# The written-out orders of five engines, laid out anew for the second part of a gated linear attention with a ReLU-gated FFN behind it

## The chip, the cores and the metric

One core of one Trainium2 chip. The metric is the device time in microseconds of one execution, the median of several runs. TensorE is called PE, VectorE DVE, ScalarE ACT, GpSimd POOL, and SyncE, whose only work here is to issue DMAs, SP.

## The reference

Four batches, eight heads, 768 time steps, head width 48. For each batch and head a state of 48 x 48 decays by a gate and takes up one outer product per step; the query reads it. The result, 3072 rows of 384, goes through an FFN of width 1536 whose gate is a ReLU.

```python
f = 1.0 / (1.0 + np.exp(-f_logit))
for t in range(S):
    state = f[:, :, t, :, None] * state + np.einsum('bhd,bhe->bhde', k[:, :, t], v[:, :, t])
    y[:, :, t] = np.einsum('bhd,bhde->bhe', q[:, :, t], state)
x = y.transpose(0, 2, 1, 3).reshape(B * S, H * D)
out = (np.maximum(x @ w_gate, 0.0) * (x @ w_val)) @ w_out
```

## The kernel before

**Tiles.** The recurrence is computed in chunks of 128 steps: inside a chunk as masked products of scaled q and k, between chunks through the state. A tile is one chunk of one batch; there are 24, in six groups of four. Tiles of groups 0 and 1 take two neighbouring chunks of the same batch together; from group 2 on a group is one chunk c of all four batches b. The FFN works on a group at a time, 512 rows, in 12 slices of its width (j = 0 to 11).

**Operations and their names.** Every operation is one entry of a plan, with a name, the buffers that it reads and writes, and the engines that can do it. For tile cb (group c, position b):

- L: a load of f, k, q or v by DMA; `Lk3.2` is k of chunk 3 for batches 2 and 3 (384 KB).
- ef, ln (ACT): the gate's logarithm. cum (PE, L503): its running sum. eq, ek, dc (ACT, from the sum's PSUM bank): the exponentials that scale q and k, and the decay.
- hq, hk (POOL or DVE): scaled q and k. xh (SP): a crossbar transpose of both by DMA. v (POOL, DVE or ACT): v in its padded layout.
- s (PE, L584): scores, here of two tiles at once into four PSUM banks (s30 is for tiles 30 and 31). m (DVE, L592): four masks for two tiles (m300, m301 for tile 30; m310, m311 for tile 31), each 128x512.
- y (PE, L752 and L756): the result of a tile, from the old state and from the masked scores; it needs both masks of its tile. kv (PE, L772), ss (DVE), sd (POOL or DVE): the new state.
- n (ACT or DVE, L597): y copied out of PSUM. xx (SP, L616): its crossbar transpose, into xT.
- g, u (PE, L792): gate and value products of one slice of a group (`g20.3`: group 2, slice 3), three matmuls each; they need the xT of all four tiles. r (ACT L797 or DVE L798): ReLU. p (DVE, L800): the product, into gT.
- o (PE, L813): output products of a tile over four slices (`o20.4`: slices 4 to 7), which need those p. d (ACT or DVE): copy out of PSUM. S (SP, L823): the store.

**What sets the order.** `ORDER` gives each engine the list of operation indices that it runs, in that order; `~60100` and the like on PE are fillers (matmuls on zeros). `BANKS` gives the PSUM bank, out of eight, of each accumulation in the order of PE. `link` and `lay_out` find the dependencies: a reader waits for its writers, a writer for earlier readers of the same buffer, and an operation that opens a bank for everything that still reads the last tenant. An engine waits at an operation until all of these are done, and what stands behind it on that engine waits too; that holds for the queue of SP, where a load behind a store or a transpose is not issued before them. The lists come from a planner outside the kernel, which lays them out by assumed durations; the durations stand in the code (`dve_`, `act_`, the pair in `by(...)`, the two numbers in `dma(...)`), but at run time nothing reads them. Only `ORDER`, `BANKS` and the dependencies act.

**Buffers that matter here.** Three output buffers (osb), so d of one tile waits for the store three tiles earlier; two xT; four places for loads of f and of v, five for k and for q.

**Two parts.** In the first (to about 56 us) tiles of groups 0 and 1 are computed; the second part begins with `g10.0` on PE, at 55.6 us.

Of the kernel before, what the change touches and what calls it, by code (L numbers as in the profile page):

```python
# [68 lines left out]
    ],  # L69
# [46 lines left out]
class Plan:  # L116
# [5 lines left out]
    def add(self, name, ways, reads=(), writes=(), key=0.0, opens=(), after=(), follows=()):  # L122
        op = Op(len(self.ops), name, ways, reads, writes, opens, key, after, follows)
        self.ops.append(op)
        return op
# [116 lines left out]
def bass_hgrn2_outer__then__ffn_reglu_kernel(  # L242
# [10 lines left out]
    B, H, S, D = q.shape  # L253
# [32 lines left out]
    osb = [sb(f"osb{i}", [128, DM], F32) for i in range(NO)]  # L286
# [13 lines left out]
    add = pl.add  # L300
    gp, ve, sc, te, sy = nc.gpsimd, nc.vector, nc.scalar, nc.tensor, nc.sync
# [20 lines left out]
    def by(e, emit, t):  # L322
        return {e: (emit, t[0], t[1], "")}
# [479 lines left out]
    def ffn_out(g, b):  # L803
        gi, oi = g % NG, (g * B + b) % NO
        P = (g + 1) * B * 10 + 5 + NJ * 3 + b * 3
        last = g == NC - 1 and b == B - 1
        cuts = [(0, 256), (256, DM)] if last else [(0, DM)]
        for x, (e0, e1) in enumerate(cuts):
# [8 lines left out]
            odst = osb[oi][:, e0:e1]  # L817
# [4 lines left out]
            dst = bass.AP(tensor=out.tensor, offset=(bt * S + ch * C) * DM + e0, ap=[[DM, C], [1, e1 - e0]])  # L822
            op = add(f"S{g}{b}" + "ab"[x] * last, by("SP", lambda odst=odst, dst=dst: sy.dma_start(dst, odst), (0.36, 0.36)), [f"osb{oi}_{x}"] + ([f"osb{oi}_1"] if x == 0 and not last else []),  # L823
# [119 lines left out]
```

## Time and profile before

| | us |
|---|---|
| median of three runs | 196.28 |
| the runs | 195.69, 196.28, 198.73 |
| the profiled execution | 197.44 |
| its span, first to last instruction | 195.7 |
| granted clock of TensorE | 1.00 throughout |

| stage (us from the span's start) | PE busy | DVE busy | ACT busy | DMA share |
|---|---|---|---|---|
| 55.4 to 79.4 (24.0) | 23.69 | 19.96 | 15.97 | 0.91 |
| 79.4 to 86.0 (6.6) | 5.72 | 5.17 | 4.12 | 0.66 |
| 86.0 to 110.2 (24.2) | 22.90 | 19.73 | 11.38 | 0.94 |
| 110.2 to 140.0 (29.8) | 28.97 | 22.45 | 12.96 | 0.97 |
| 140.0 to 169.5 (29.5) | 28.42 | 19.42 | 9.28 | 0.50 |
| 169.5 to 195.7 (26.2) | 23.27 | 13.35 | 5.54 | 0.16 |

A matmul's busy time contains its way through the array, which overlaps with the next one, so a busy PE can still lose time between two matmuls; the distance between starts tells it. The DMA share is the mean over 16 DMA engines of the time that their packets took, and can exceed 1 where packets overlap. A load of 384 KB issued by SP lands between 5.1 and 5.9 us after its issue at the median, the transpose into xT after 2.7, the transpose of scaled q and k after 3.6, a store after 2.2.

### The profile page before, as it was taken

How to read it: one execution, taken by the hardware profiler on the slowest of the kernel's cores; microseconds unless marked ns; L12 is line 12 of the kernel's file. 1: busy time of each engine (PE TensorE's matmuls, PEld its weight loads, DVE VectorE, ACT ScalarE, POOL GpSimd, SP SyncE). 2: the span in 40 equal slices, each digit the busy share in tenths (PEclk: the TensorE clock that was granted, in tenths of full speed). 3: DMA queues.
4: the chain of work that ended last, by engine and by line, in shares of the span. 5: the costliest groups of instructions: out<-in, count | busy, mean ns of one | idle time of the engine just before them, and what ended most of it. 6: DMA issues, size and time to landing. Idle time of an engine off the chain costs nothing.

```text
span 195.7 us, 4619 instructions
## 1 busy us (share of the span) xinstructions
PE 185.2 (95%) x1858; PEld 109.7 (56%) x1881; DVE 141.1 (72%) x266; ACT 88.4 (45%) x190; POOL 53.7 (27%) x83
## 2 busy tenths in 40 slices
PE   7998999999999999989989898999998999999994
PEld 7554675555655556655555455566544556555563
DVE  4486947997859797877896767997348976277621
ACT  2776962511689923464227684226077012122120
POOL 8858402901407830106121705014006000000000
PEclk9999999999999999999999999999999999999999
DMA  6999999999999895969998799995593711410013
GB/s 152 325 284 208 153 201 269 213 214 283 245 202 223 191 164 114 202 149 197 222 218 178 154 232 143 238 224 117 156 284 71 111 40 24 163 59 0 0 46 118
DMA packets 113638, 33.21 MB, mean 170 GB/s; under 512 B 106832, under 2 KB 113360, under 8 KB 113616
## 3 DMA queue, kind: packets, MB, share of 16 engines
q1 hardware_dynamic: 102576, 27.01, 63.9%
q0 software_dynamic: 3776, 3.54, 11.5%
q10 hardware_dynamic: 7264, 2.36, 4.6%
q8 instruction: 15, 0.25, 0.5%
q14 instruction: 7, 0.06, 0.1%
HBM read 25.95 MB, written 4.72 MB: 157 GB/s over the span
## 4 chain that ended last, share of the span: by engine, by line
PE 66%; DMA 11%; DVE 8%; ACT 6%; issue 4%; SPq 2%; POOL 1%; DVEq 0%; ACTq 0%
PE ps L792 34%; PE ps L813 20%; DMA f_in<-in_f_logit_dram 9%; DVE gT L800 4%; DVE relu L798 2%; PE ps L584 2%; DMA xT<-xn 2%; PE ps L756 1%; PE ps L752 1%; PE ps L503 1%; ACT relu L797 1%; ACT expo L516 1%; ACT expo L518 1%; PE ps L672 1%; DVE hats L541 1%
## 5 line engine op out<-in xcount | busy, mean ns | idle before, releaser
L800 DVE TENSOR_TENSOR gT<-relu,ps 128x512 bf16<-128x512 bf16 (+1 forms) x76 | 48.8, 654 | 19.7 <-ACT relu L797 10.9
L792 PE MATMUL ps<-xT,wg 128*128 128x512 bf16 (+1 forms) x218 | 56.0, 368 | 2.2 <-DMA xT<-xn 1.6
L792 PE MATMUL ps<-xT,wv 128*128 128x512 bf16 (+1 forms) x219 | 56.2, 368 | 0.5
L813 PE MATMUL ps<-wo,gT 128*128 128x384 bf16 (+2 forms) x300 | 51.8, 320 | 0.0
L797 ACT ACTIVATE relu<-ps 128x512 bf16<-128x512 f32 (+1 forms) x43 | 24.9, 582 | 49.2 <-DVE gT L800 24.1
L813 PEld LDWEIGHTS ps<-wo,gT 128*128 128x128 bf16 x300 | 27.4, 98 | 17.4 <-DVE gT L800 0.6
L792 PEld LDWEIGHTS ps<-xT,wv 128*128 128x128 bf16 x228 | 23.6, 108 | 19.9
L792 PEld LDWEIGHTS ps<-xT,wg 128*128 128x128 bf16 x228 | 23.1, 108 | 20.4 <-DMA xT<-xn 1.9
L540 POOL TENSOR_TENSOR hats<-q_in,expo 128x384 bf16<-128x384 f32 x15 | 15.6, 1050 | 39.8 <-ACT expo L518 28.6
L798 DVE TENSOR_SCALAR relu<-ps 128x512 bf16<-128x512 f32 (+1 forms) x33 | 21.0, 645 | 3.9 <-PE ps L792 3.5
L592 DVE TENSOR_TENSOR ptm<-ps,tri 128x512 bf16<-128x512 f32 x32 | 20.7, 682 | 2.9 <-PE ps L584 2.8
L820 DVE COPY osb<-ps 128x384 f32<-128x384 f32 (+1 forms) x14 | 7.5, 536 | 12.2 <-PE ps L813 6.7
L570 POOL CAST vpad<-v_in 128x384 bf16<-128x384 f32 x9 | 5.0, 562 | 38.1 <-DMA v_in<-in_v_dram 38.1
L540 POOL TENSOR_TENSOR hats<-k_in,expo 128x384 bf16<-128x384 f32 x12 | 12.0, 1011 | 12.1 <-ACT expo L516 11.9
L819 ACT ACTIVATE osb<-ps 128x384 f32<-128x384 f32 (+1 forms) x11 | 5.3, 478 | 21.9 <-PE ps L813 15.4
L478 ACT ACTIVATE f_in<-f_in 128x768 f32<-128x768 f32 x12 | 10.1, 841 | 8.1 <-DMA f_in<-in_f_logit_dram 8.1
L518 ACT ACTIVATE expo<-ps 128x384 f32<-128x384 f32 x24 | 11.6, 493 | 2.9 <-PE ps L498 1.6
L516 ACT ACTIVATE expo<-ps 128x384 f32<-128x384 f32 x24 | 11.6, 492 | 2.4 <-POOL hats L540 1.7
L597 ACT ACTIVATE xn<-ps 128x384 bf16<-128x384 f32 x11 | 5.3, 487 | 14.0 <-PE ps L756 14.0
L877 PE MATMUL ps<-zeros 128*128 128x100 bf16 (+1 forms) x80 | 11.0, 310 | 0.5 <-issue 0.3
L657 DVE TENSOR_TENSOR ptm<-ps,tmask 128x512 bf16<-128x512 f32 x16 | 10.1, 681 | 0.2 <-PE ps L650 0.2
L481 ACT ACTIVATE bneg<-f_in 128x768 bf16<-128x768 f32 x12 | 10.1, 841 | 0.2
(74 smaller groups left out, 170.9 us busy)
## 6 DMA issues: line engine op xcount, KB each, us to landing
f_in<-in_f_logit_dram SPq DMA_DIRECT2D x12, 384.0 KB, 5.9
out_dram<-osb SPq DMA_DIRECT2D x23, 192.0 KB, 2.2
q_in<-in_q_dram SPq DMA_DIRECT2D x11, 384.0 KB, 5.6
k_in<-in_k_dram SPq DMA_DIRECT2D x11, 384.0 KB, 5.6
v_in<-in_v_dram SPq DMA_DIRECT2D x8, 384.0 KB, 5.1
v_in<-in_v_dram ACTq DMA_DIRECT2D x4, 384.0 KB, 7.6
wg<-in_moe_w_gate_dram POOLq DMA_DIRECT2D x2, 384.0 KB, 8.2
wv<-in_moe_w_val_dram POOLq DMA_DIRECT2D x2, 384.0 KB, 8.4
```

Source lines behind the costliest of these rows:

```text
L478: add(f"ef{c}{b0}", by("ACT", lambda: sc.activation(raw, raw, AF.Exp, scale=-1.0), act_(n)), keys, keys, key=P)
L481: add(f"ln{c}{b0}", by("ACT", lambda: sc.activation(bo, fl, AF.Ln, bias=1.0), act_(n)), keys + [f"bneg{bi}"], [f"bn{bi}_{x % 2}" for x in ...
L516: add(f"ek{c}{b}", by("ACT", lambda: sc.activation(ex[:, 1, :], bc.ap[:, 0:HD], AF.Exp, scale=1.0), act_(HD)), [bc], [f"expk{ei}"], key=P + 1)
L518: add(f"eq{c}{b}", by("ACT", lambda: sc.activation(ex[:, 0, :], bc.ap[:, 0:HD], AF.Exp, scale=-1.0), act_(HD)), [bc], [f"expq{ei}"], key=P ...
L540: return {**by("POOL", lambda: gp.tensor_tensor(o, i_, e_, ALU.mult), pool_(HD)), **by("DVE", lambda: ve.tensor_tensor(o, i_, e_, ALU.mult ...
L592: add(f"m{c}{b}{j}", by("DVE", lambda b=b, j=j, mi=mi: ve.tensor_tensor(ptm[mi][:, j, :, :], s[b, j].ap[:, :].rearrange("p (n t) -> p n t" ...
L792: z = te.matmul(bank.ap[:, 0:n], wt[:, kt, w_cols(j)], xT[xi][:, kt, n0:n1], start=(kt == 0), stop=(kt == NK - 1))
L797: add(f"r{c}{b0}.{j}", {**by("ACT", lambda: sc.activation(rdst, gate.ap[:, 0:n], AF.Relu), act_(n)), **by("DVE", lambda: ve.tensor_scalar_ ...
L798: **by("DVE", lambda: ve.tensor_scalar_max(rdst, gate.ap[:, 0:n], 0.0), dve_(n))}, [gate], [f"relu{ri}"], key=P)
L800: add(f"p{c}{b0}.{j}", by("DVE", lambda: ve.tensor_tensor(gT[gi][:, j, n0:n1], rdst, val.ap[:, 0:n], ALU.mult), dve_(n)), [val, f"relu{ri} ...
L813: z = te.matmul(o.ap[:, 0:e1 - e0], gT[gi][:, j, b * C:(b + 1) * C], wo[:, j, e0:e1], start=(j == 0), stop=(j == NJ - 1))
L877: te.matmul((op.opens[0].ap if op.opens else banks[7])[:, 0:fill % 1000], zeros[:, 0:128], zeros[:, 0:fill % 1000], start=True, stop=True, ...
```

## The change

`ORDER` and `BANKS` are replaced from a certain place on each engine; up to there every list is the same. On PE the first place that differs stands behind `g10.0`, where `u10.0` comes in front. On SP it stands behind `Lf2.2` and `S00`, where `S02` comes in front of `Lq2.0`. 79 operations move to another engine, most of them between ACT and DVE: relu 17 from ACT to DVE and 14 back, copies of y 6 and 3, output copies 3 and 7. No operation is added or dropped. One assumed duration changes, that of the issue of a store. Of the lists, cut to the first lines that differ on PE and SP, and the rows that hold the stretch around group 2's start:

```diff
@@ ORDER, PE
-        262, 294, 298, 215, 216, 217, 306, 308, 302, 388, 310, 380, 312, 326, 410, 322, 324, 338, 415, 423, 404, 328, 342,
+        262, 294, 298, 215, 216, 217, 306, 308, 302, 304, 388, 310, 380, 312, 326, 423, 415, 328, 342, 344, 410, 322, 404,
...
-        407, 366, 340, 351, 436, 367, 542, 352, 442, 357, 556, 360, 361, 550, 553, 362, 547, 561, 460, 452, 454, 569, 462,
+        357, 407, 431, 401, 350, 351, 442, 360, 361, 362, 436, 550, 556, 352, 542, 561, 569, 553, 547, 460, 462, 476, 478,
...
@@ ORDER, SP
-        46, 48, 50, 55, 53, 58, 64, 66, 59, 60, 65, 373, 371, 370, 374, 214, 372, 376, 516, 375, 518, 386, 224, 394, 517,
+        46, 48, 50, 55, 53, 58, 64, 66, 59, 60, 65, 373, 371, 370, 374, 214, 224, 372, 376, 516, 229, 375, 518, 394, 517,
...
@@ ffn_out
-            op = add(f"S{g}{b}" + "ab"[x] * last, by("SP", lambda odst=odst, dst=dst: sy.dma_start(dst, odst), (0.36, 0.36)), [...])
+            op = add(f"S{g}{b}" + "ab"[x] * last, by("SP", lambda odst=odst, dst=dst: sy.dma_start(dst, odst), (0.6, 0.6)), [...])
```

The stretch around the second pair of rows in names:

```
PE before: ... y20 u10.11 o11.4 s22 y21 o13.4 u10.9 o10.4 y22 o13.8 s30 o10.8 y23 o11.8 kv31 o12.0 o12.4
           kv30 y31 o12.8 y30 cum32 g20.3 g20.1 u20.1 cum33 u20.3 g20.7 ...
PE after:  ... y21 s22 y20 o10.0 o10.4 y23 o12.0 o12.4 o12.8 y22 kv30 kv31 o10.8 s30 cum32 cum33 y31 y30
           g20.3 u20.3 g20.7 u20.7 g20.11 u20.11 g20.0 u20.0 g20.4 u20.4 g20.8 u20.8 g20.2 ...
DVE before: ... m221 m230 m220 p10.9 m231 m310 m301 d10 v30 m311 ss31 m300 sd31 ss30 sd30 d13 r20.3 ...
DVE after:  ... m210 m211 m200 m201 m231 m230 m221 m220 n20 ss30 ss31 sd30 m311 m300 m310 m301 d13 n30 r20.3
            p20.3 r20.7 hk33 p20.7 r20.11 p20.11 p20.0 r20.4 p20.4 r20.8 p20.8 p20.1 p20.5 ss33 ...
ACT after:  ... d11 n21 n23 v30 v31 d12 n22 ef32 d10 ln32 eq32 dc33 dc32 eq33 ek32 n31 ek33 r20.0 ...
SP before:  ... S01 xh30 xh31 xx20 Lv3.0 xx21 Lf3.2 xx22 xx23 S10 S11 Lk3.2 Lq3.2 xx30 Lq4.0 Lv3.2 S13 xh32 xh33
            S12 xx31 Lk4.0 Lf4.0 Lv4.0 Lv4.2 xx32 xx33 Lf4.2 Lk4.2 ...
SP after:   ... S01 xh23 xh31 xh30 Lv3.0 Lf3.2 xx21 xx20 xx23 xx22 S10 Lk3.2 Lq3.2 Lq4.0 S13 xx30 Lv3.2 Lk4.0
            xh33 xh32 S12 xx31 Lf4.0 Lv4.0 Lv4.2 Lf4.2 Lk4.2 xx33 xx32 xh40 xh41 S11 Lq4.2 ...
```

Later places that the prediction speaks of, in the same way: on PE `u30.8 s40 g30.2`, then `s42 o32.0 u30.9 o31.0 y42 o30.0 u30.6 g30.10 y43 o32.4`; `cum51 cum50 o30.8 g40.1 u40.1 g40.5 u40.5 g40.9 u40.9 g40.2 cum53 cum52`; `y50 g40.7 u40.7 o43.0 s52 ... y53 o41.4 o40.8`. On SP the last load of f stands in `xx42 xx43 S22 Lf5.2 S32`, before in `S22 Lk5.0 Lf5.2 S30`. On DVE `s40`'s masks open a run `m400 m401 m410 p30.2 m411 r30.3 hq43 p30.3 r30.6 p30.7 v50 n41 p30.1 r30.11 p30.11 p30.5 m420 m421 m431 p30.9 m430 n42 p30.6`. On ACT `eq50 ek51 ek50 d30 r40.1 eq51 ef52 r40.5 ln52`. PE ends with `o53.4b o53.8b`, the half of 128 columns, where before it ended with `o53.4a o53.8a`, the half of 256.

More of the change, by code (lines that the diff above doesn't have):

```diff
@@ L822, in ffn_out @@
             dst = bass.AP(tensor=out.tensor, offset=(bt * S + ch * C) * DM + e0, ap=[[DM, C], [1, e1 - e0]])
-            op = add(f"S{g}{b}" + "ab"[x] * last, by("SP", lambda odst=odst, dst=dst: sy.dma_start(dst, odst), (0.36, 0.36)), [f"osb{oi}_{x}"] + ([f"osb{oi}_1"] if x == 0 and not last else []),
+            op = add(f"S{g}{b}" + "ab"[x] * last, by("SP", lambda odst=odst, dst=dst: sy.dma_start(dst, odst), (0.6, 0.6)), [f"osb{oi}_{x}"] + ([f"osb{oi}_1"] if x == 0 and not last else []),
                      [f"out{g}_{b}_{x}"], key=P)
```

72 rows, old and new, of tables (BANKS, ORDER) are left out of this document.

## The prediction

> **What bounds the kernel now.** I read the page first (busy shares, slices, chain), then who PE waits for from 55 us on, then the order of time around the largest wait, then the landing times of the DMAs. All durations are of the one profiled execution: span 195.7 us, 197.44 us with what lies around it; the median of the runs is 196.28 us.
>
> ```profile
> PE 185.2 (95%) x1858; PEld 109.7 (56%) x1881; DVE 141.1 (72%) x266; ACT 88.4 (45%) x190; POOL 53.7 (27%) x83
> ...
> PEclk9999999999999999999999999999999999999999
> ...
> PE 66%; DMA 11%; DVE 8%; ACT 6%; issue 4%; SPq 2%; POOL 1%; DVEq 0%; ACTq 0%
> ```
>
> PE sets the end at an undisturbed clock; the 11% of DMA on the chain is mostly the first load of f, which the change doesn't touch.
>
> ```profile
> PE ps L792 <- DMA xT<-xn: 1.6, 2, 0.9
> PE ps L503 <- ACT bneg L481: 0.9, 1, 0.9
> PE ps L584 <- DVE ssum L454: 0.5, 1, 0.5
> PE ps L584 <- DVE relu L798: 0.4, 1, 0.4
> PE ps L792 <- issue: 0.4, 2, 0.2
> PE ps L772 <- DVE hats L541: 0.2, 1, 0.2
> ```
>
> In the second part PE visibly waits 4.0 us, and 1.6 + 0.9 of it is for transposes and for a late load of f. A second count gives what reordering can win at all. The chain has `88.14 6.51 PE ps L792 x30`, 0.217 us a matmul, so a gate or value piece (3 matmuls) is 0.65 us; in the same way an output piece (4) is 0.65, a score piece s 0.55, y 0.37, a state product kv 0.17, a cumulative sum 0.26 (0.16 in batch 5). From g10.0 (55.6 us) to the last matmul there are 118 gate/value pieces (76.3 us at 0.647), 57 output pieces and the two narrow halves (37.1 + 2.0), 8 s (4.4), 16 y (6.0), 12 kv (2.0) and 16 sums (3.8): 131.6 us, to 187.2. The last matmul ends at 193.0, so some 5.8 us is lost. No order of the same work gains more, and a gain of over 2% (3.9 us) needs two thirds of it back.
>
> ```profile
> 79.45 0.62 PE L584 MATMUL ps<-qkT 48*128 48x128 bf16 x16
> 79.47 3.46 SPq L616 DMA_TRANSPOSE xT<-xn  x2
> ...
> 80.11 1.29 DVE L592 TENSOR_TENSOR ptm<-ps,tri 128x512 bf16<-128x512 f32 x2 [0.92 <-PE ps L584]
> ...
> 82.05 0.68 DVE L592 TENSOR_TENSOR ptm<-ps,tri 128x512 bf16<-128x512 f32 x1
> ...
> 83.11 0.68 DVE L592 TENSOR_TENSOR ptm<-ps,tri 128x512 bf16<-128x512 f32 x1
> ...
> 83.32 0.33 PE L752 MATMUL ps<-st,qkT 128*128 128x96 bf16 x4
> ...
> 84.34 0.33 PE L752 MATMUL ps<-st,qkT 128*128 128x96 bf16 x4
> ...
> 86.01 0.38 PE L792 MATMUL ps<-xT,wg 128*128 128x512 bf16 x1 [0.89 <-DMA xT<-xn]
> ```
>
> First s30, then its four masks on DVE, then y31 and y30, which read them, then g20.3, held by xx23. Between s30's end and y31 PE has 3.2 us of other work here: that hides the masks. The last transpose takes 3.99 us to land (chain: `81.75 3.99 DMA xT<-xn`); the median is 2.7, between 2.3 and 5.2.
>
> **The change part by part.** No instruction is added or removed. The 0.36 that becomes 0.6 at L823 is a planner's cost; the orders are written out, so it runs as nothing. 79 operations change engine: DVE takes 17 relu from ACT and gives 14 back, and ends 5 instructions up, some 3 us of busy time. What counts is where PE meets a wait.
>
> *Waits that go.* ln52 and cum53 (0.9): Lf5.2 was issued at 140.19, behind Lk5.0, and landed 5.03 later. Now it stands behind xx43 and S22, some 8 us of PE work ahead of cum53; 5.0 of landing, 0.9 for exp and 0.9 for log leave about a microsecond, though r40.1, eq51 and r40.5 share ACT with them. g30.1 (0.7): its transposes had 5.2 us of PE work from the last y of the batch, now 7.2. s32 (0.5): from cum32 and cum33 it had 10.0, now 14.5. s40 and kv43 (0.4 + 0.2): their places change, with slack. g50 keeps its 5.2 us, but n53 follows y53 directly. With the 0.4 of "issue" this is 3.1 of the 4.0. The 0.9 before g20.3 goes too, but see the next.
>
> *The wait that comes.* The new order of PE is y22, kv30, kv31, o10.8, s30, cum32, cum33, y31, y30, g20.3: only 0.52 us between s30 and y31, where 3.2 stood. Let s30 start at t. DVE has ss30, ss31 and sd30 (0.55 each) from kv30's result at t - 0.65, so until t + 1.0; s30's result is there at t + 0.7. Then m311, m300, m310, m301, 0.68 each: m310 ends at t + 3.05, m301 at t + 3.73. PE reaches y31 at t + 1.07 and waits 2.0; y31 takes 0.37, and y30 waits 0.3 more. g20.3 starts at t + 4.15 instead of t + 1.81: 2.3 us. Its transposes: y20's copy n20 stands behind eight masks on DVE, at about t - 2.0, then xx20, xx23 and xx22 leave SP 1.2 apart, xx22 at t + 0.45; at the median it lands at t + 3.15, hidden, at 3.99 it lands at t + 4.4 and costs 0.3. I take the median, because Lf3.2, which stood between xx21 and xx22 before, now stands ahead of all four.
>
> The Trainium skill (DMA: Bandwidth & Descriptors, Queues, rings and completion order) says that an engine takes descriptors of a ring in their order, so a load issued ahead delays a transpose. By that rule the move of Lf3.2 is right and the sum stays; the five loads that now stand ahead of xx33 would go against it, by up to the 1.3 between 3.99 and 2.7. Row and order: those five (384 KB each) need some 10 us at the 200 GB/s that the slices show, and g30.1 is 17 us of work away.
>
> *Where DVE falls behind.* From kv21 to y20 I followed ACT and DVE with the same durations: kv20 waits 0.3 for dc21 (ACT has r10.6, dc22, ek22 ahead of it), o13.0 0.25 for p10.3, o13.4 0.45 for p10.4 (p10.11, p10.5, r10.4, hq30 ahead, 2.6 us of DVE), s20, s22 and y20 0.5 together: 1.5, where this stretch lost 0.8. From s40 to o32.4 DVE has no gap: 23 instructions, 15 us, and p30.6 comes 0.6 late for o32.4. In batch 4, y50 waits 0.2 (m501), o43.0 0.3 (p40.3), o40.8 0.4 (p40.11, behind n52 and r40.11). Four further places (g10.5, s40, o32.0, u30.9) have under 0.15 us of slack; a wait that ends just in time showed 0.2 here, so I count 0.4.
>
> *Sum.* New order: 1.5 + 2.3 + 0.15 (o20.4 on p20.6) + 0.6 + 0.9 + 0.4 = 5.9, against 5.8 lost now. At the end the last copy and store are 128 columns wide instead of 256: copy 0.29 for 0.38, landing 1.6 for 1.7, 0.2 less. Span 195.6. My slack is read from busy times that ignore semaphores, which errs towards too little waiting, so I add 0.2 and leave the tail out: 195.8, or 196.4 beside the median.
>
> **The rivals.** *A, the later landing pays in full (0.14):* DVE reaches the masks early and the pinch costs 0.5 or less. Then the sum of 5.9 falls by 1.8, and without the 0.4 to 3.7, 2.1 less than is lost now; with the tail's 0.2 that is a span of 193.4 and a time of 194.0. For it: DMA is the last releaser at two of the largest waits. Against: four masks in a row are 2.7 us whatever the DMAs do.
>
> *B, slower: a load stops DVE (0.13).* hk33 now stands on DVE between r20.7 and p20.7, with all of batch 2's relu and products behind it. It needs Lk3.2, issued only after S10, about 5 us ahead of it. k loads land in 5.7 at the median, but between 3.7 and 12.1. PE goes on until u20.8 wants the bank of p20.7, some 2.4 us of slack. It decides from a landing of about 7.4 us; at 12.1 PE loses 4.7: 201.1. For it: S02 and S03 also now stand ahead of Lq2.0 and Lk2.2, and S03 waits for d03 on DVE, so these leave 1 to 3 us later. Against: Lk3.2 before, issued at 85.28, let hk32 start at 89.18, after 3.9.
>
> *C, the clock (0.03).* The trace grants full clock in all 40 slices; its longest wait of PE in the second part is 0.9, the new ones 2.0 and 0.3. If one slice of 4.9 us ran at half, 2.45 us of work is lost: 198.9. The Trainium skill (TensorE: Matmul & The Clock Gate, Why this matters for your kernels) warns of idle gaps over some 3 us; by that rule 2.0 stays short of it, and no run here shows a longer one.
>
> **How the numbers follow.** The likeliest case has 0.70, at 196.4, with its own range 194.6 to 198.6: the transpose's 0.3, the tight places and a pinch between 1.0 and 3.0. To hold 8 in 10 I reach down into A and towards C: 193.6 to 199.2. 2% is about what a measurement of this kernel can tell from no change (its runs lie between 195.69 and 198.73): faster is under 192.4, slower over 200.2. Faster needs A with most of the short waits gone as well: 0.06. Slower is B beyond a landing of 11.2 us (half of its chance, 0.06) or lags of DVE that add up in the likeliest case (0.06): 0.12. Within 2%: 0.82.
>
> **What would show it.** Right: a wait of PE for DVE ptm at L756 or L752 of about 2 us near 86, none for xT at g20.3 over 0.4, none for bneg at L503 of 0.9, and PE's last matmul within 2 us of 193. Wrong: hk33 idle for k_in with PE idle behind it (B); no wait at y31 (A); a clock under 9 (C); or a new wait on xT or qkT.

## The result and the profile after

| | before | after |
|---|---|---|
| median, same chips (us) | 197.37 | 198.30 |
| the runs (20 each) | 195.69 to 199.02 | 196.86 to 199.14 |
| profiled execution, its span | 197.44, 195.7 | 198.99, 197.2 |
| g10.0 starts, last matmul ends (us of the span) | 55.61, 193.01 | 56.61, 194.81 |

The ratio after to before is 1.0055, 95% interval 1.0030 to 1.0079: the change costs about 1.1 us, where I had forecast practically none (196.4 beside 196.28). The comparisons leave out executions more than 1.5% above the fastest of their kernel; that matters most for one control, before with two loads on ACT, where it takes out eight of twelve, the profiled one among them.

In the profile the second part, from g10.0 to the end of the last matmul, takes 138.2 us against 137.4. The other 1.0 us of the profiled pair lies ahead of g10.0, where PE's list is the same: over all profiles of this study g10.0 starts between 55.6 and 57.0 us, so I don't count it.

The page of after: busy times, the granted clock, and the chain that ended last, by engine.

```profile
PE 184.8 (94%) x1861; PEld 108.7 (55%) x1881; DVE 145.0 (74%) x271; ACT 87.0 (44%) x187; POOL 51.9 (26%) x81
...
PEclk9999999999999999999999999999999999999999
...
PE 41%; DMA 25%; DVE 14%; ACT 10%; SPq 3%; POOL 3%; issue 3%; DVEq 0%; ACTq 0%
```

PE holds 41% of the chain where it held 66%: what ended last now runs for longer stretches through DMA, DVE and ACT. Who PE waits for in after, from 55 us on (us in total, times, longest):

```profile
PE ps L503 <- ACT bneg L481: 3.4, 3, 1.4
PE ps L752 <- DVE ptm L592: 0.4, 1, 0.4
PE ps L792 <- issue: 0.2, 1, 0.2
PE ps L813 <- DVE gT L800: 0.2, 1, 0.2
```

Of the six lines of before two are left, one of them grown. The 1.6 us for xT are gone, and so are the waits of s32, s40 and kv43. In their place stand three waits of a running sum for the logarithm of f: cum32 (1.05 us by the distance of starts), cum41 (1.56) and cum53 (1.22). In order of time the last two are:

```profile
108.72 0.34 PE L503 MATMUL ps<-bneg,tri 128*128 128x384 bf16 x1 [1.40 <-ACT bneg L481]
...
149.12 0.50 PE L503 MATMUL ps<-bneg,tri 128*128 128x384 bf16 x2 [1.06 <-ACT bneg L481]
```

The bracket is the idle time of the engine. Where I give a wait by the distance of starts, it is the time from the start of the operation before, less what that operation takes where nothing waits. For cum53 that is 0.65 us, seen in two of the kernels below. The texts written before the runs count cum53's waits 0.2 us lower.

**The pinch at the start of group 2.** Order of time in after, first PE, then DVE; the bracket is the idle time before, and who ended it.

```profile
84.64 0.62 PE L584 MATMUL ps<-qkT 48*128 48x128 bf16 x16
86.24 0.32 PE L503 MATMUL ps<-bneg,tri 128*128 128x384 bf16 x1 [0.98 <-ACT bneg L481]
...
87.26 0.34 PE L752 MATMUL ps<-st,qkT 128*128 128x96 bf16 x4 [0.36 <-DVE ptm L592]
...
87.86 0.34 PE L752 MATMUL ps<-st,qkT 128*128 128x96 bf16 x4
...
88.46 0.59 PE L792 MATMUL ps<-xT,wg 128*128 128x512 bf16 x2
...
85.33 2.48 DVE L592 TENSOR_TENSOR ptm<-ps,tri 128x512 bf16<-128x512 f32 x4
```

s30, cum32, y31, y30 and g20.3. The first of g20.3's three matmuls is missing from the trace; its weight load shows when it began:

```profile
88.22 0.33 PEld L792 LDWEIGHTS ps<-xT,wg 128*128 128x128 bf16 x3
```

From s30 to g20.3 it is 3.82 us to the first recorded matmul, so about 3.60 to its real start, for 1.81 of work. (Waits at g20.3 and g40.1 below are counted to the real start in the same way.) cum32 is held by ln32 first, then the four masks hold y31. No line of PE names xT, but it was close: xx22 landed at 88.18.

**cum41.** ACT in after, ef40 and ln40:

```profile
106.95 0.84 ACT L478 ACTIVATE f_in<-f_in 128x768 f32<-128x768 f32 x1 [3.49 <-DMA f_in<-in_f_logit_dram]
107.83 0.84 ACT L481 ACTIVATE bneg<-f_in 128x768 bf16<-128x768 f32 x1
```

Lf4.0 was issued at 102.30 (before: 98.93) and landed at 106.93 (before: 104.89). Counted from g10.0 it left SP 2.4 us later than in before and landed 1.0 later, while PE came to cum41 0.8 earlier, and in before ln40 ended only 0.3 ahead of PE. ACT sat idle for the load and PE reached cum41 1.56 us too early.

**cum53.** ACT in after, from d31 to ln52:

```profile
144.23 0.49 ACT L819 ACTIVATE osb<-ps 128x384 f32<-128x384 f32 x1 [3.66 <-PE ps L792]
...
146.95 0.90 ACT L478 ACTIVATE f_in<-f_in 128x768 f32<-128x768 f32 x1
...
148.16 0.90 ACT L481 ACTIVATE bneg<-f_in 128x768 bf16<-128x768 f32 x1
```

The bracket names PE, but what d31 needs of PE, o31.8, started at 141.71 and takes 0.65. d31 also needs its output buffer, which store S22 was reading: S22 stands behind xx42 and xx43 on SP, was issued at 141.91 and landed at 144.15, 0.08 us ahead of d31:

```profile
138.84 3.02 SPq L616 DMA_TRANSPOSE xT<-xn  x2
141.91 0.57 SPq L823 DMA_DIRECT2D out_dram<-osb  x1
```

All of ACT's list up to ef52 and ln52 stands behind d31. Lf5.2 had landed at 146.18, and ef52 began only at 146.95: about 0.8 of cum53's 1.22 us is d31's, the rest the landing of Lf5.2. In before S22 held d31 as well (landing 141.66, start 141.74), but there ef52 waited for Lf5.2 itself (landing 145.22, start 145.25).

**Where SP's stream lost time.** Both kernels in the window 78 to 89 us: length, then busy time (instructions) of PE, PEld, DVE, ACT and POOL, granted clock, DMA share, GB/s. Before:

```profile
78.00:89.00 11.00, 10.11 (x123) 6.61 (x122) 8.80 (x16) 6.29 (x16) 0.50 (x1) 1.00 0.83 180
```

After:

```profile
78.00:89.00 11.00, 9.55 (x151) 6.81 (x151) 7.47 (x14) 7.18 (x19) 1.08 (x1) 1.00 0.48 105
```

Before, n20 was written early and xx20 left SP at 75.29. In after SP stands still from 77.78 to 79.25 for n21 and from 80.43 to 82.26 for n20, which DVE copies behind eight masks. Nothing behind them can be issued, so the DMA engines move 105 GB/s instead of 180. From there to about 138 us SP issues nearly without a pause, and Lf4.0 and Lf5.2 leave late: 2.4 us and 1.3 us later than in before, counted from g10.0.

### The profile page after: what moved, and what is told of

Read it like the earlier page. It is cut to its first block, busy times and chain, and to the rows that moved or that the text cites. A ratio compares the mean times of both kernels' runs of the same rounds, so it can differ in the third digit from the quotient of the medians.

```text
span 197.2 us, 4621 instructions
## 1 busy us (share of the span) xinstructions
PE 184.8 (94%) x1861; PEld 108.7 (55%) x1881; DVE 145.0 (74%) x271; ACT 87.0 (44%) x187; POOL 51.9 (26%) x81
## 3 DMA queue, kind: packets, MB, share of 16 engines
q10 hardware_dynamic: 7264, 2.36, 4.6%
## 4 chain that ended last, share of the span: by engine, by line
PE 41%; DMA 25%; DVE 14%; ACT 10%; SPq 3%; POOL 3%; issue 3%; DVEq 0%; ACTq 0%
PE ps L792 19%; PE ps L813 16%; DMA f_in<-in_f_logit_dram 8%; DMA k_in<-in_k_dram 5%; DMA v_in<-in_v_dram 5%; DVE gT L800 5%; DMA wg<-in_moe_w_gate_dram 3%; DMA wo<-in_moe_w_out_dram 2%; DVE ptm L592 2%; POOL hats L540 2%; ACT f_in L478 2%; ACT relu L797 2%; ACT expo L516 2%; DVE relu L798 2%; SPq L616 2%
## 5 line engine op out<-in xcount | busy, mean ns | idle before, releaser
L797 ACT ACTIVATE relu<-ps 128x512 bf16<-128x512 f32 (+1 forms) x40 | 23.3, 583 | 38.9 <-PE ps L792 22.2
L798 DVE TENSOR_SCALAR relu<-ps 128x512 bf16<-128x512 f32 (+1 forms) x36 | 23.1, 648 | 4.8 <-PE ps L792 4.1
L819 ACT ACTIVATE osb<-ps 128x384 f32<-128x384 f32 (+1 forms) x15 | 7.3, 485 | 31.7 <-PE ps L813 27.1
L540 POOL TENSOR_TENSOR hats<-q_in,expo 128x384 bf16<-128x384 f32 x10 | 10.8, 1082 | 31.9 <-ACT expo L518 19.2
L540 POOL TENSOR_TENSOR hats<-k_in,expo 128x384 bf16<-128x384 f32 x13 | 13.2, 1030 | 19.9 <-ACT expo L516 14.3
L820 DVE COPY osb<-ps 128x384 f32<-128x384 f32 (+1 forms) x10 | 5.2, 528 | 13.8 <-PE ps L813 9.9
L456 POOL TENSOR_TENSOR st<-ssum,dec 128x384 bf16<-128x384 f32 x9 | 7.6, 858 | 18.9 <-DVE ssum L454 18.9
L541 DVE TENSOR_TENSOR hats<-q_in,expo 128x384 bf16<-128x384 f32 x14 | 8.0, 579 | 4.7 <-ACT expo L518 4.7
L454 DVE TENSOR_TENSOR ssum<-ps,st 128x384 f32<-128x384 f32 x16 | 8.6, 551 | 2.6 <-PE ps L772 1.7
L597 ACT ACTIVATE xn<-ps 128x384 bf16<-128x384 f32 x8 | 3.9, 490 | 14.7 <-PE ps L756 14.7
```

The costliest lines, as they stand in the source:

```text
L454: add(f"ss{c}{b}", by("DVE", lambda: ve.tensor_tensor(tmp[:, :], kv.ap[:, 0:HD], s_old[:, :], ALU.add), dve_(HD)), [kv, f"S{b}_{(c + 1) % ...
L540: return {**by("POOL", lambda: gp.tensor_tensor(o, i_, e_, ALU.mult), pool_(HD)), **by("DVE", lambda: ve.tensor_tensor(o, i_, e_, ALU.mult ...
L541: **by("DVE", lambda: ve.tensor_tensor(o, i_, e_, ALU.mult), dve_(HD))}
L797: add(f"r{c}{b0}.{j}", {**by("ACT", lambda: sc.activation(rdst, gate.ap[:, 0:n], AF.Relu), act_(n)), **by("DVE", lambda: ve.tensor_scalar_ ...
L798: **by("DVE", lambda: ve.tensor_scalar_max(rdst, gate.ap[:, 0:n], 0.0), dve_(n))}, [gate], [f"relu{ri}"], key=P)
```

## The experiments

Theory: the change took the xT waits away and got them back as waits for f, since all of SP's entries form one stream; its order only decides which landing comes last, and time lost while SP stands at a late copy comes out at later loads. Rivals: single entries stand in the wrong place (then one move pays), or the masks on DVE, or the engines' new orders whatever SP does. In the diffs the entries of `ORDER` are written as names. Ratios are to before on the same chip.

### How far before repeats

The kernel before once more: 198.54 us, span 196.7.

> The kernel before once more, for a second profile. In the two profiles at hand g10.0 starts at 55.8 (before) and 56.8 (after) although the orders up to there are the same; four further kernels with that front had it between 55.9 and 56.7. If this is the spread of one kernel from run to run, g10.0 comes anywhere from 55.5 to 57.0 here and the stages behind it take what they took in the first profile within 0.7 us (137.2 from g10.0 to the last matmul). If the front differs by cause, it is at 55.8 within 0.2.

g10.0 starts at 55.59, as in the first profile, which doesn't decide the question of the front. The second part took 138.4 us against 137.4: 1.0 more, beyond the 0.7 that I expected, and as much as after took with 138.2. So one pair of profiles can't show a difference of 0.8 us; only the runs show that after is slower. g20.3 waited 0.63 for xT, s32 1.15, cum53 1.50 (first profile, same count: 0.82, 0.64, 1.08). Single waits differ by half a microsecond between two executions of one kernel; a profile shows which waits there are, the runs how much they are worth.

### One entry of SP moved ahead

```diff
 SP (Lf4.0 ahead):  xh33 xh32
-  S12 xx31 Lf4.0 Lv4.0
+  Lf4.0 S12 xx31 Lv4.0
```

> The changed kernel with one entry of SP moved: Lf4.0 goes ahead of S12 and xx31, two places earlier. In the changed kernel it is issued at 102.30, lands at 106.93, and cum41 waits 1.4 for ln40. Theory (a load of f that stands too late in SP's queue takes the place of the transposes as the last releaser): issue near 100.5, ln40 1.8 earlier, the wait of L503 for bneg at 108.7 gone or under 0.2, 1.0 to 1.5 us less, ratio to the kernel before about 0.999. Rival (the DMA engines are full, so a load issued earlier lands no earlier): wait and time as in the changed kernel, ratio 1.0055. Rival (what stands behind takes it back: hk40, v40 or the transposes xx33 and xx32): the wait goes, the time falls by under 0.4 and a wait of another name appears before 125.

1.0044 [1.0008, 1.0081]. The wait at cum41 is gone. In its place s32 waits 0.45 us for a state sum on DVE, o21.0 1.24 for p20.2 and g40.1 0.53 for xT; cum53 keeps its 1.22.

```diff
 SP (S22 ahead):  Lf5.0 Lk5.2
-  xx41 xx40 Lv5.2 Lk5.0 xx42 xx43 S22 Lf5.2
+  S22 xx41 xx40 Lv5.2 Lk5.0 xx42 xx43 Lf5.2
```

> The changed kernel with one entry of SP moved: the store S22, whose data is ready since about 115, goes ahead of xx41, from behind xx43. In the changed kernel S22 is issued at 141.9, lands at 144.15, the copy d31 takes its buffer at 144.23, and the exponentials of group 5, ef52 and ln52 stand behind d31 on ACT; cum53 waits 1.06. Theory (a store late in SP's queue holds ACT through the output buffer): d31 starts at about 142, ef52 when Lf5.2 has landed at about 145.7, the wait of L503 at 149.1 falls to 0.2 or less, 0.7 to 1.0 us less. Rival (the landing of Lf5.2 holds ef52): d31 earlier, but ef52 and the wait at cum53 move by under 0.3.

1.0016 [0.998, 1.0051]. d31 starts at 142.40 instead of 144.23, as soon as PE gives its data, so S22 did hold it. The wait at cum53 is gone too, but this alone doesn't show that d31 made it: PE came later, having lost 2.0 us at g40.1, and ef52 started right behind Lf5.2's landing (146.91 behind 146.79), which counted from g10.0 is 0.6 later than in after. PE's waits in this kernel:

```profile
PE ps L503 <- ACT bneg L481: 2.5, 2, 1.5
PE ps L792 <- DMA xT<-xn: 2.1, 1, 2.1
```

The 2.1 us are g40.1's: xx43, now behind S22, landed at 145.14 instead of 142.98.

```diff
 SP (Lf5.2 ahead):  Lv5.2 Lk5.0
-  xx42 xx43 S22 Lf5.2
+  Lf5.2 xx42 xx43 S22
```

> The changed kernel with one entry of SP moved: Lf5.2 goes ahead of xx42, xx43 and S22. It would be issued at about 138.9 instead of 142.5 and land some 3 us earlier; S22 comes 0.5 later. Theory (the store S22 holds ACT): d31 and all behind it on ACT are 0.5 later, ef52 at 147 or later, the wait at cum53 stays at 1.0 to 1.5, no gain, 0 to 0.5 us more. Rival (the landing of Lf5.2 holds ef52): the wait at cum53 goes, 0.8 to 1.0 us less.

1.0131 [1.0093, 1.0169], the worst of the single moves. Lf5.2 landed at 142.38, 3.8 earlier, and cum53 still waited 1.22: S22 landed at 145.00, d31 started at 145.09 and ef52 only at 147.81, behind it. With the load early, the store alone is enough for the whole wait. g40.1 waited 0.91 on top. Of two causes in a row, removing the one that was not last bought nothing and cost the other its place.

```diff
 SP (Lk3.2, Lq3.2 into the gaps at n21 and n20):  Lv3.0 Lf3.2
-  xx21 xx20 xx23 xx22 S10 Lk3.2 Lq3.2 Lq4.0
+  Lk3.2 xx21 Lq3.2 xx20 xx23 xx22 S10 Lq4.0
```

> The changed kernel with two entries of SP moved: Lk3.2 ahead of xx21 and Lq3.2 ahead of xx20, into the stretch from 77.8 to 82.3 in which SP waits 1.5 for n21 and 1.8 for n20 and the DMA engines carry 105 GB/s (0.48 of their time from 78 to 89, against 0.83 and 180 GB/s before the change). Theory (the waits of PE in the middle come from one stream of loads and transposes; what it loses in front of a copy that comes late, all later loads are late by): S10 follows xx22 at once and everything on SP behind it is 1.5 to 2 earlier, Lf4.0 is issued near 100.4, the wait of L503 near 108 falls under 0.3, 1.0 to 1.8 us less, ratio about 0.998. Rival (the stream does not bind; order only swaps which wait comes last): Lf4.0 lands earlier, but other waits take its place, under 0.4 us. Rival (loads ahead of transposes delay xT): g20.3 waits 0.5 to 1.5 more for xT, time the same or up to 1 us more.

1.0039 [0.9992, 1.0086]. The gap is filled, the wait at cum41 gone, cum53's 0.85. But the transposes now run among the loads, xx20 takes until 87.69 to land (84.58 in after), and g20.3 waits 0.85 for xT. The profiled execution (197.48 us) kept the full clock; nine of the twelve did not (mean 0.983 to 0.991, median 199.8 us), so the profile alone doesn't explain the ratio.

### The pinch

```diff
 ACT (ln32 early):  d11 n21 n23 v30 v31
-  d12 n22 ef32 d10 ln32 eq32
+  ef32 d12 n22 ln32 d10 eq32
```

> The changed kernel with two entries of ACT moved: ef32 ahead of d12 and ln32 ahead of d10. In the changed kernel cum32 waits 1.0 for ln32, y31 0.5 and y30 0.2 for the masks, g20.3 0.2 for xT. Theory (the four masks and, behind them, the transposes set the start of g20.3; ln32 is only the first wait in front): the wait at cum32 falls to 0.3 or less and those at y31 and y30 grow by as much; g20.3 starts at the same distance from s30, 3.8, time unchanged within 0.3 us. Rival (ln32 sets it): 0.8 us less.

1.0054 [1.0032, 1.0076]. cum32's wait is gone and y31 waits 1.53 instead; s30 to the first recorded matmul of g20.3 is 3.82 us, as in after. So the masks set the pinch, and ln32's wait lies inside it.

```diff
-DVE: ... m221 m220 n20 ss30 ss31 ...
+DVE: ... m221 m220 ss30 ss31 ...
-ACT: ... d11 n21 n23 ...
+ACT: ... d11 n21 n20 n23 ...
```

> The changed kernel with the copy n20 done by ACT behind n21 instead of by DVE behind eight masks. It ends near 80.1 instead of 82.23, so xx20 is issued at 80.45 instead of 82.26. Theory (the late copy holds SP and with it the stream): the gap of 1.8 on SP closes in part, xx22 is issued when n22 is done (84.3 instead of 84.8), S10 and all behind it 0.5 to 1.0 earlier, 0.3 to 1.0 us less, the wait near 108 shrinks by as much. Rival (the masks set the start of g20.3 and no load is reached sooner, because xx22 waits for n22 anyway): under 0.3 us.

1.0053 [1.0013, 1.0094]. cum53's wait fell to 0.48, cum41's 1.57 stayed, and s30 to g20.3 took 3.82 again, counted in the same way. One copy less on DVE doesn't move the masks.

### SP's order alone, and the rest without it

After with SP's list of before, and before with SP's list of after (only S33 put back behind S43, which before's other lists need):

```diff
 after, SP list replaced by that of before:
-  xh31 xh30 Lv3.0 Lf3.2 xx21 xx20 xx23 xx22 S10 Lk3.2 ...
+  xh30 xh31 xx20 Lv3.0 xx21 Lf3.2 xx22 xx23 S10 S11 Lk3.2 ...
```

> After, with SP's order of before; all other engines' orders as in after. Theory of the stream (SP's one queue sets the landings, and a copy that is late for its transpose stops it): in SP's order of before xx20 stands ahead of Lv3.0, xx21 and Lf3.2, and in after n20 is written at 82.2 us behind eight masks, so SP waits some 5 us there (77 to 82), Lf3.2 and all later loads land 3 to 5 us later than in after, cum32 and later cum41 wait for ln: ratio 1.015 to 1.03 to before. Rival (the engines' new orders alone cost the 0.55%, what SP does with them is of no weight): 1.004 to 1.008, and SP's order is exchangeable.

1.1034 [1.0987, 1.1082]; 219.2 us. SP in order of time (SPq is its issuing):

```profile
74.73 1.31 SPq L560 DMA_TRANSPOSE qkT<-hats  x1
81.68 1.18 SPq L616 DMA_TRANSPOSE xT<-xn  x1
82.91 0.58 SPq L411 DMA_DIRECT2D v_in<-in_v_dram  x1
...
85.44 0.58 SPq L411 DMA_DIRECT2D f_in<-in_f_logit_dram  x1
```

Here SP stands for 5.6 us at xx20, and Lv3.0 and Lf3.2 leave 7.6 and 9.5 us later than in after. PE waits 4.15 us at kv30 for v30 and 1.33 at cum32, as the theory says. But its price was far too low: I had priced the first stop alone, and others follow, the longest of 9.5 us at a transpose of scaled q and k. A part of the 21 us is clock: its mean was 0.958 in this profile.

```diff
 before, SP list replaced by that of after:
-  xh30 xh31 xx20 Lv3.0 xx21 Lf3.2 xx22 xx23 S10 S11 Lk3.2 ...
+  xh31 xh30 Lv3.0 Lf3.2 xx21 xx20 xx23 xx22 S10 Lk3.2 ...
```

> Before, with SP's order of after (S33 alone put back behind S43, since before's other engines need it there). Theory of the stream: in before n20 and n21 are written early (by ACT, ahead of the loads' queue), so SP doesn't stand still at them and the loads behind land early; what changes is that xx20 comes after Lv3.0, Lf3.2 and xx21, so the xT wait ahead of g20.3 grows by 0 to 1.5 us, and the waits of the loads of f shrink: 0.995 to 1.006. Rival (the new order of SP is bad in itself, or the new orders only pay together): 1.01 or more, with a new wait of over 1.5 us.

1.0637 [1.059, 1.0684], what the rival said: the lists only pay together. g20.3 waits 1.27 for xT, g30.7 3.20 for the output copy d20 (on DVE, which over the whole run sits 13.0 us idle for stores ahead of such copies), cum50 3.80 for ln50; the mean clock was 0.968. Both swaps show that the lists of one kernel are fitted to each other and neither can be changed back alone. They don't divide the 0.55% between them.

### Off the queue

Two loads issued by ACT, whose list has room behind n21, in place of SP:

```diff
-SP:  ... xx22 S10 Lk3.2 Lq3.2 Lq4.0 ...
+SP:  ... xx22 S10 Lq4.0 ...
-ACT: ... d11 n21 n23 ...
+ACT: ... d11 n21 Lk3.2 Lq3.2 n23 ...
```

> The changed kernel with Lk3.2 and Lq3.2 issued by ACT behind n21 (about 79.3 and 79.8, where ACT idles 2.2) instead of by SP. Theory (the time that SP needs to issue is what is short, 1.2 for each transpose): SP's own list is 2 us shorter from 87.7 on, gain as in the fill of SP's gap or 0.3 more, 1.0 to 2.0 us less. Rival (the 16 DMA engines are what is short): the same gain as from the fill, within 0.3. Rival (ACT is held by the issue, as some issues on SP take up to 3.5): n23 and with it xx23 and xx22 come later, g20.3 waits for xT, no gain.

0.9969 [0.9928, 1.0009]. The loads are issued at 78.24 and 78.65, while SP waits; the DMA share of 78 to 89 us is 0.93, cum41's wait is gone, and unlike in the kernel with the two loads in SP's own gaps the transposes still arrive in time. Left are cum32's 1.05, o21.0's 0.92 for p20.2 and cum53's 0.86.

The last two hang on stores: d13 on DVE waits 2.58 us for the landing of S10, with n30, r20.3 and the products up to p20.2 behind it, and d31 waits for S22. So these two stores go to ACT as well:

```diff
 (with the two loads on ACT)
-SP:  ... xx22 S10 ... xx42 xx43 S22 Lf5.2 ...
+SP:  ... xx22 ... xx42 xx43 Lf5.2 ...
+ACT: ... ef32 d10 ln32 S10 eq32 ... d22 dc43 S22 dc42 ...
```

> After, with Lk3.2 and Lq3.2 issued by ACT behind n21 as in the run that gave 0.9969, and the two stores S10 and S22, which hold d13 on DVE and d31 on ACT through the output buffers, issued by ACT too (S10 behind ln32, S22 behind dc43). If late stores and the stream are what is left: d13 starts 1 to 2 us earlier and the 0.92 us wait of o21.0 for p20.2 goes, d31 no longer waits for the landing of S22, and cum53's 0.65 us becomes 0.2 to 0.6 (Lf5.2 still lands near 144.5): ratio 0.988 to 0.995. Rival (the time of issue on ACT, 0.4 to 2 us each, delays ACT's own chain, or another landing takes the place): 0.995 to 1.003.

**0.9899 [0.9854, 0.9943]**, 196.19 us against 198.66: better than both kernels. Its waits of PE:

```profile
PE ps L503 <- ACT bneg L481: 1.0, 1, 1.0
PE ps L752 <- DVE ptm L592: 0.4, 1, 0.4
PE ps L792 <- issue: 0.2, 1, 0.2
PE ps L813 <- DVE gT L800: 0.2, 1, 0.2
```

The pinch is left, and 0.2 us at cum53. S22 landed at 115.85 instead of 144.15, d31 started at 140.21, Lf5.2 landed at 143.59. From s32 to g30.1, the stretch of cum41, it is 12.83 us instead of 14.57; from g10.0 to the start of o53.8b 134.97 instead of 137.81, a difference of 2.84 us. The ratios differ by 1.56%, or 3.1 us.

The stores alone, loads back on SP:

```diff
-SP:  ... xx22 S10 Lk3.2 Lq3.2 ... xx42 xx43 S22 Lf5.2 ...
+SP:  ... xx22 Lk3.2 Lq3.2 ... xx42 xx43 Lf5.2 ...
+ACT: ... ln32 S10 eq32 ... dc43 S22 dc42 ...
```

> After, with only the two stores S10 (behind ln32) and S22 (behind dc43) issued by ACT; Lk3.2 and Lq3.2 are back on SP. The combined kernel gave 0.9899, the two loads alone 0.9969, after 1.0053. If the stores' landings, which hold d13 and d31, and the stream's lateness are two separate causes: the waits of o21.0 and most of cum53's 1.0 us go, cum41's 1.57 us stays at 1.0 to 1.6: ratio 0.996 to 1.001. Rival (it is the number of entries on SP alone, whichever they are): S10 and S22 stand behind Lf3.2 and in part behind Lf4.0, cum41's wait also falls below 0.8 us, ratio 0.990 to 0.996.

1.0021 [0.9987, 1.0055]. The waits at cum53 and at cum41 both went. d31 started at 141.80 and ef52 right behind the landing of Lf5.2 (145.66 behind 145.64), counted from g10.0 1.1 earlier than in after. Lf4.0 was issued at 101.51, 0.6 earlier counted from g10.0, and took 3.55 us to land instead of 4.63, so one entry less ahead of it was enough here, as the rival said. But g20.3 now waits 1.20 for xT (xx22 landed at 89.22, beside S10 from ACT) and g40.1 0.60; the ratio lies above both expectations. Loads and stores together gain 1.56%, either alone 0.86% and 0.34%; the intervals are too wide to say that the whole is more than its parts.

### The same in the kernel before

```diff
-SP:  ... S10 S11 Lk3.2 Lq3.2 xx30 ...
+SP:  ... S10 S11 xx30 ...
-ACT: ... n21 n22 n23 d11 ...
+ACT: ... n21 n22 n23 Lk3.2 Lq3.2 d11 ...
```

> Before, with Lk3.2 and Lq3.2 issued by ACT behind n23 in place of SP. Theory of the stream (any entry taken off SP in this stretch makes all later landings earlier, whichever kernel): Lf4.0 and Lf5.2 are issued 0.8 to 1.5 us earlier, ratio 0.993 to 0.999, as 0.9969 against 1.0055 was gained in after. Rival (the two loads helped in after alone, since there SP stood waiting for n20 while they could have been issued): 0.999 to 1.004, with the waits of before in their places.

0.9973 [0.9921, 1.0025]. The interval reaches from below the theory's range to above 1 and so decides nothing; all twelve lie between 196.55 and 202.29 with a median of 199.99, above before's 198.66. Four executions had a mean clock of 1.000 and took 196.55 to 199.47; the other eight, at 0.983 to 0.991, took 199.56 to 202.29. The profile (199.56 us, mean clock 0.991) shows that the theory's mechanism failed: counted from g10.0, Lf4.0 left SP not 0.8 to 1.5 us earlier than in before but 1.5 later, and g20.3 waits 2.42 us for xT. Here SP was not standing still, the two loads run against the transposes, and xx23 took 5.8 us to land instead of 3.99. So no gain is shown. That two such loads pay only where the queue stands fits this pair of kernels, and rests on it alone.

```diff
-SP:  ... xx43 S23 S22 Lk5.0 Lf5.2 ...
+SP:  ... xx43 S23 Lk5.0 Lf5.2 ...
+ACT: ... ef42 ln42 S22 r30.7 ...
```

> Before, with the one store S22 issued by ACT behind ln42 in place of SP. In before d31 on ACT waits 6.03 us for the landing of S22, and cum53 waits 1.29 us. If the held output buffer is a cost of both kernels: cum53's wait falls to 0 to 0.8 us (Lf5.2's own landing at 145.2 is the other cause), ratio 0.993 to 0.999, and the slack that stores give is none of the change's doing. Rival (in before Lf5.2's landing alone sets cum53, as it lands 145.22 and ef52 begins at 145.25): 0.998 to 1.002, the wait stays above 1 us.

1.0013 [0.9981, 1.0044]. d31 starts at 141.27, as soon as PE gives its data, and the wait at cum53 is gone, as the first expectation said, but for another reason: PE came about 1 us later, as cum50 waits 0.51 for ln50 and s32 0.96. ef52 started at 145.31, right behind the landing of Lf5.2 (145.29), as in before (145.25 behind 145.22). So the earlier d31 changed nothing for ef52: the rival's cause and its time hold. That the late store cost before anything is not shown.

### The pinch once more, in the best kernel

```diff
 (with loads and stores on ACT)
-DVE: ... m221 m220 n20 ss30 ...
+DVE: ... m221 m220 ss30 ...
-ACT: ... n21 Lk3.2 Lq3.2 n23 v30 v31 d12 n22 ef32 d10 ln32 S10 ...
+ACT: ... n21 Lk3.2 Lq3.2 n20 n23 v30 v31 ef32 d12 n22 ln32 d10 S10 ...
```

> The kernel that gave 0.9899 (after with Lk3.2, Lq3.2, S10, S22 on ACT), and in it n20 copied by ACT behind Lq3.2 in place of DVE, ef32 moved ahead of d12 and ln32 ahead of d10. What is left there is the mask pinch: cum32 1.05 us for ln32 and y31 0.50 us for m310. If DVE's row of eight masks and n20 sets y31: with n20 gone from DVE (0.48 us) and ln32 early, s30 to g20.3 falls from 3.82 to 3.2 to 3.5 us: ratio 0.986 to 0.990. Rival (the masks for y31 are late whatever stands beside them, or what ACT gains at ln32 it loses by n20): 0.989 to 0.995, s30 to g20.3 at 3.7 us or more.

0.9933 [0.9905, 0.9962], not better than without these moves. y31 waits 1.53 for m310, and g20.3 0.65 for xT. s30 to g20.3 is 4.47 us by the recorded matmuls, beyond the rival's 3.7, and the clock falls behind it (last section). Half of the twelve executions had a mean clock of 0.991, with a median of 197.3 us, the others 0.999 to 1.000 and 196.3. The pinch is the row of masks, and I found no cheap move that shortens it.

## Why the prediction was wrong, point by point

- **The pinch** (2.3 us): right. It is 1.8. y31 came 2.62 us after s30 (I had 3.05), y30 3.22 (3.73), g20.3 3.60 (4.15). That ln32 would hold cum32 for 1.05 of it I hadn't seen; it costs nothing, as ln32 moved early showed. The four masks took 2.48 us in a row where I had 2.72.
- **xT hidden at the median**: right, just so. xx22 landed less than 0.1 us ahead of g20.3, which is luck more than margin. The Trainium skill's ring order (DMA: Bandwidth & Descriptors, Queues, rings and completion order) would have been against the five loads ahead of xx33; g30.1 doesn't wait for xT in after, so for g30.1 it cost nothing.
- **Waits that go**: right for xT, s32, s40 and kv43; **wrong for ln52 and cum53**, and this is the step that failed. I wrote that Lf5.2 "stands behind xx43 and S22, some 8 us of PE work ahead of cum53" and found about a microsecond to spare. The wait stayed: 1.22 us where I had 0. I had followed the load alone. S22 beside it is also what frees d31's buffer, and d31 stands ahead of ef52 on ACT. In after ef52 began 0.77 us behind the landing of its load; with Lf5.2 put ahead of S22 the wait stayed at 1.22, behind d31; with S22 on ACT ef52 ran right behind the landing, and in the best kernel 0.2 of the wait is left.
- **A wait that I never listed**: cum41 for ln40, 1.56 us. Counted from g10.0 Lf4.0 was issued 2.4 us later than in before. My sum has no term for it, so this too was put at nothing. I asked of each load what stands ahead of it in the list, not whether SP issues on time: n20 "behind eight masks on DVE" is in my working, as a matter of xT's landing only. That SP, and with it every later load, stands there too, I did not carry on. Putting Lf4.0 two places ahead removed the wait, taking two loads off the queue at that place did, and so did two stores less.
- **Where DVE falls behind**: too large. The early stretch lost 0.7 (I had 1.5), s40 to o32.4 0.15 (0.6), batch 4 0.3 (0.9), the tight places nothing I could find (0.4). My count of busy times erred towards too much waiting, the opposite of what I added 0.2 for.
- **The sum**: 5.9 forecast; by the same count 6.6 (138.2 us from g10.0 on, less 131.6). About 2.3 too much for DVE and 0.5 too much for the pinch nearly cancel 2.8 too little for loads of f. That the sum is off by only 0.7 is luck: the errors have opposite signs. The 0.7 that remain are small waits that I did not place. The 0.8 us between the first two profiles is of the size of the 1.1 us that the runs show, but before's second profile took as long as after's, so the runs alone carry the difference.
- **The rivals**: A did not come, since the pinch was there. B did not come: hk33 ran at 92.33 without a gap on DVE, Lk3.2 having landed at 91.47. C did not come in after's profile, where the clock is full in all slices; in five of the twenty executions of after the mean clock was 0.991, but their median, 198.31 us, is that of the other fifteen (198.29), so C doesn't carry the 1.1 us.

What stays open: how much of the 1.1 us each wait is worth in the mean over runs, and how much of it in the other kernels is clock. Moving the waits one at a time put others in their place, so only their sum with the queue relieved is measured: 3.1 us from after to the best kernel, of which the profiles place 1.56 at cum41, 1.0 at cum53 and about 0.3 in small waits.

## What to carry to other kernels

Read a queue of transfers as an engine of its own: for each entry ask when its data is ready, and charge the time that it stands there to everything behind it, up to the end of the stretch in which the queue has no pause. A store has a reader behind it, too: follow its buffer to the next writer and to what stands behind that writer. Moving one entry ahead in a full queue traded one wait for another here; what paid in this kernel was to use the time in which the queue stands, from a queue that doesn't.

## What the runs showed of the hardware

**A second queue runs past a standing one.** In after SP stood still 1.8 us for n20. The same loads issued by ACT left meanwhile: Lk3.2 at 78.24, landing at 83.12 instead of 91.47. In the best kernel the page shows loads and stores of ACT on q10, the queue that carries ACT's few loads in after too, 11680 packets against 7264:

```profile
q10 hardware_dynamic: 11680, 3.54, 7.4%
```

But the transfers still meet each other: where SP was not standing, the same two loads made g20.3 wait 2.42 us.

**A transpose holds its queue.** In after each xx or xh kept SP for 1.2 to 1.3 us, 96 KB or 256 KB alike, and up to 2.9 us where entries stood close; a load kept it 0.4 to 0.6 us, or 1.1 to 3.5 us in such stretches.

**The clock fell after short waits.** The kernel with n20 and ln32 moved, in windows of 4 us (columns as above, the clock after POOL):

```profile
84.00:88.00 4.00, 2.38 (x51) 1.78 (x50) 3.22 (x6) 3.46 (x11) 1.69 (x2) 0.97 0.90 178
88.00:92.00 4.00, 3.47 (x11) 1.53 (x13) 2.57 (x5) 0.13 (x1) 2.29 (x3) 0.61 0.40 106
```

PE had waited 1.5 and 0.65 us close together, and the clock was 0.61 in the next 4 us. In before with two loads on ACT a single wait of 2.42 us was followed by 0.60:

```profile
88.00:92.00 4.00, 2.35 (x6) 1.02 (x8) 1.25 (x2) 0.99 (x3) 0.00 (x0) 0.60 1.09 265
```

After the 4.15 us wait of after with SP's old list it was 0.50 from 87 to 95. Yet the stores-alone kernel, with waits of 1.05, 0.49 and 1.20 in 5 us, kept 1.00, and six of twelve executions of the first kernel named here kept 0.999 or more. The Trainium skill (TensorE: Matmul & The Clock Gate, HAM oscillation — how this bites in real kernels) speaks of idle gaps over about 3.4 us; the 4.15 agrees, the 2.42 alone and the 1.5 with 0.65 came sooner. Four us at 0.61 are 1.6 us of work at the full clock, so a pinch of 2 us can cost nearly as much again; what decides whether it does these runs don't show.
